# The order of seven Strassen products and their additions, with a PSUM bank as one resource in the plan

## The chip, the cores and the metric

The kernel runs on one core of a Trainium2 chip. The metric is the device time of one execution in microseconds (us). TensorE does the matrix products into PSUM (eight banks of 512 fp32 values in each of 128 partitions), VectorE and ScalarE read and write PSUM and SBUF, GpSimd works on SBUF alone here, and SyncE issues the DMAs.

## What is computed

Linear attention with random features, and then two two-layer perceptrons on its 2304 x 512 result:

```python
k_p, q_p = phi(k * scale), phi(q * scale)          # exp features, 128 of them
kv, z = einsum('bhsm,bhsd->bhmd', k_p, v), k_p.sum(axis=2)
x = (q_p @ kv) / (q_p @ z + 1e-6)                  # 4 x 8 heads, 576 tokens
h = x @ w_in;  x = (h * tanh(softplus(h))) @ w_out     # first perceptron, d_ff 2048
h = x @ w_in2; x = (h * sigmoid(h)) @ w_out2           # second perceptron
```

All inputs and outputs are fp32. Each product runs as three fp32r matmuls on a high and a low part (`mm3`, lines 202 to 205).

## The kernel before

Every instruction is a task of a plan (class `Plan`, lines 69 to 190). A task has an engine, a cost, a due key, names that it reads and writes, and rings of buffers from which it opens new tiles. `order` is a greedy list scheduler: it follows the modelled time, and on the engine that can start first it takes, among the tasks that can start within 0.1 us of that, the one with the lowest key. A reader becomes ready when the last writer's modelled end plus a latency has passed (`LAT`: 0.2 us behind TensorE, 0.15 behind ScalarE and VectorE), a writer behind the last writer and all readers. The list that comes out fixes the order of instructions on every engine. The waits themselves (semaphores) are set afterwards by the tile framework from the tiles' real accesses, not by the plan.

The tokens go in blocks of 256. In the first stretch (attention and phase 0, up to about 395 us) the products `h`, `y`, `kpj`, `qpj` and others run without Strassen. From then on each block of 512 tokens (phases 1 to 4) goes through pairs of 128-wide slices of d_ff. One pair is a step, `step(s, st)` from line 698. Its first layer is a 2 x 2 Strassen-Winograd product: seven products instead of eight, each of six 256-column matmuls (lines 734 to 744), with additions afterwards. A step uses:

- bank A (`ha`) and bank B (`hb`), each 512 columns wide, left half 0 and right half 1; the ring `h4` has four banks, so two steps fit;
- `u`, a tile in SBUF (named `Lfz` in the trace, after the space that it reuses);
- `uz` (ScalarE, line 765): copies B's right half to `u` 0; `ua`, `ub`, `uc`, `ud`, `ue` (VectorE, line 759): u0 += A left; u1 = u0 + B left; B right = u1 + A right; A right = u0 + A right; B left = u0 + B left;
- `act` (lines 705 to 710): the activation `e` (ScalarE, L707), its high part `gh` (ScalarE, L708), its low part `gl` (VectorE, L709), for A and for B; `gh` and `gl` have two buffers each;
- the second layer `Y` (lines 785 to 820): four pieces for a step, two for A's half and two for B's, each of six 512-column matmuls into the `y` banks (a ring of four other banks). Evacuation at a block's end is L841 or L843.

Products are called by their operand number v: in the names of the plan product 4 of step 7 is `Ma7.4`. Before the change the plan's names for what a product writes are `ha:0`, `ha:1`, `hb:0`, `hb:1`, that is, one for each half. Keys: products 0, 4, 5, 3 have the step's key, products 1, 2, 6 with `ud`, `ue` and the activations 0.6 more, `Y` 2.6 more (and an offset of 1.1 for `Y`); the next step's key is 1.9 higher. The last block of 256 tokens has its own branch (`N == 256`, lines 746 to 753) with four products into one bank.

Beside the steps, weights of later pairs are converted and split (`to_f32` and `conv_pair`: ScalarE L612 and L632, VectorE L614 to L618 and L651, GpSimd L633), and the operands of each block are loaded and combined (`load_x`: DMA, VectorE L877).

Of the kernel before, what the change touches and what calls it, by code (L numbers as in the profile page):

```python
# [13 lines left out]
ALU = mybir.AluOpType  # L14
# [179 lines left out]
def performer_two_mlps(ctx: ExitStack, tc: tile.TileContext, qin, kin, omT, w1, w2, out):  # L194
    nc = tc.nc
    PE, ACT, DVE, POOL = nc.tensor, nc.scalar, nc.vector, nc.gpsimd
# [5 lines left out]
    def mm3(o, s_hi, s_lo, m_hi, m_lo, first, last):  # L202
        PE.matmul(o, s_hi, m_hi, start=first, stop=False, skip_group_check=True)  # L203
        PE.matmul(o, s_lo, m_hi, start=False, stop=False, skip_group_check=True)  # L204
        PE.matmul(o, s_hi, m_lo, start=False, stop=last, skip_group_check=True)  # L205
# [61 lines left out]
    T = plan.add  # L267
# [59 lines left out]
    def om_prep():  # L327
# [6 lines left out]
      new=[("cst", "cst")], lat=D)  # L334
# [363 lines left out]
    def step(s, st):  # L698
        ph, N, s_ = st["ph"], st["N"], st["key"]
        pair = "p" in st  # L700
        gh, gl = [f"gh{s}.{x}" for x in range(2)], [f"gl{s}.{x}" for x in range(2)]
        AFN = AF.Mish if ph < 2 else AF.Silu
        tab = "M" if ph < 2 else "S"

        def act(x, h, res, ks):
            e = f"e{s}.{x}"
            T(f"X{s}.{x}", "ACT", 0.6, ks, lambda: ACT.activation(t[e], t[h], AFN), reads=res, writes=[e], new=[(e, "e")], tab=tab)  # L707
            T(f"gh{s}.{x}", "ACT", 0.62, ks, lambda: ACT.copy(t[gh[x]], t[e]), reads=[e], writes=[gh[x]], new=[(gh[x], "ghi")])  # L708
            T(f"gl{s}.{x}", "DVE", 0.69, ks, lambda: DVE.tensor_tensor(t[gl[x]], t[e], t[gh[x]].bitcast(F32), ALU.subtract),  # L709
              reads=[e, gh[x]], writes=[gl[x]], new=[(gl[x], "glo")])  # L710

        if not pair:
            h, X = f"h{s}", f"X{st['bi']}"
            xres = [f"{X}:{x}{g}" for x in "hl" for g in range(2)]

            def H(f, k):
                whi, wlo = [ap() for _, ap in wt_[f, 0]]
                for c in range(NCC):
                    mm3(t[h][:, k * N:(k + 1) * N], whi[:, c * P:(c + 1) * P], wlo[:, c * P:(c + 1) * P], t[X][:, 0, c, :], t[X][:, 1, c, :],
                        c == 0, c == NCC - 1)  # L720

            for k, f in enumerate(st["fs"]):
                T(f"H{s}.{k}", "PE", 1.41, s_, lambda f=f, k=k: H(f, k), reads=xres + [x for x, _ in wt_[f, 0]],
                  writes=[h], new=[(h, "h")] if not k else [])
            act(0, h, [h], s_)
            g_of = [(0, k * N) for k in range(2)]
            wout = [([x for x, _ in wt_[f, 1]], lambda f=f: [ap() for _, ap in wt_[f, 1]]) for f in st["fs"]]
        else:
            p = st["p"]
            V = [f"V{p}.{v}" for v in range(7)]  # L730
            xv = f"x{min(ph, 3) if ph < 4 else 4}.{st['bi']}."
            wout = [([f"O{p}.{x}h", f"O{p}.{x}l"], lambda x=x: [t[f"O{p}.{x}h"], t[f"O{p}.{x}l"]]) for x in range(2)]

            def product(o, v, b, first, last):

                m = [t[xv + b + x].rearrange("p (c t) -> p c t", t=256) for x in "hl"]
                for c in range(2):
                    mm3(o, t[V[v]][:, c * P:(c + 1) * P], t[V[v]][:, 256 + c * P:256 + (c + 1) * P], m[0][:, c, :], m[1][:, c, :],
                        first and c == 0, last and c == 1)

            def M(nm, h, x, v, b, first, last, new, ks, extra=()):
                T(f"M{nm}{s}.{v}", "PE", 0.703, ks, lambda: product(t[h][:, x * 256:(x + 1) * 256], v, b, first, last),
                  reads=[V[v] + ":h", V[v] + ":l", xv + b + "h", xv + b + "l"], writes=[f"{h}:{x}"],
                  new=[(h, "h4")] if new else [], after=extra)

            if N == 256:
                h = f"h{s}"
                M("a", h, 0, 0, "11", True, False, True, s_, ["att"])
                M("a", h, 0, 1, "21", False, True, False, s_)
                M("a", h, 1, 3, "11", False, False, False, s_, [f"Ma{s}.0"])  # L750
                M("a", h, 1, 2, "T", False, True, False, s_)
                act(0, h, [h + ":0", h + ":1"], s_)
                g_of = [(0, k * N) for k in range(2)]
            else:
                A, B, u = f"ha{s}", f"hb{s}", f"u{s}"
                q = lambda r, x: t[r][:, x * 256:(x + 1) * 256]

                def add(nm, o, ox, a, ax, b, bx, ks, new=()):
                    T(f"{nm}{s}", "DVE", 0.42, ks, lambda: DVE.tensor_tensor(q(o, ox), q(a, ax), q(b, bx), ALU.add),  # L759
                      reads=[r for r in (f"{a}:{ax}", f"{b}:{bx}") if r != f"{o}:{ox}"], writes=[f"{o}:{ox}"], new=list(new))  # L760


                M("a", A, 0, 0, "11", True, False, True, s_, ["att"])
                M("a", B, 1, 4, "T2", True, True, True, s_)
                T(f"uz{s}", "ACT", 0.37, s_, lambda: ACT.copy(q(u, 0), q(B, 1)), reads=[B + ":1"], writes=[u + ":0"], new=[(u, "u")])
                add("ua", u, 0, u, 0, A, 0, s_)
                M("a", B, 0, 5, "T3", False, False, False, s_, [f"Ma{s}.4"])
                add("ub", u, 1, u, 0, B, 0, s_)
                M("a", A, 1, 3, "T1", False, False, False, s_, [f"Ma{s}.0"])
                add("uc", B, 1, u, 1, A, 1, s_)  # L770
                M("b", A, 0, 1, "21", False, True, False, s_ + 0.6)
                M("b", B, 0, 2, "T4", False, True, False, s_ + 0.6)
                M("b", A, 1, 6, "22", False, True, False, s_ + 0.6)
                add("ud", A, 1, u, 0, A, 1, s_ + 0.6)
                act(0, A, [A + ":0", A + ":1"], s_ + 0.6)
                add("ue", B, 0, u, 0, B, 0, s_ + 0.6)
                act(1, B, [B + ":0", B + ":1"], s_ + 0.6)
                g_of = [(0, 0), (1, 0)]

        tail = s == len(steps) - 1  # L780
        nb = NCC if tail or (ph == 4 and N == 256) else NCC * N // DM
        Y_ = [f"y{ph}.{st['bi']}.{i}" for i in range(nb)]
        epb = NCC // nb

        def Y(k, cs):
            whi, wlo = wout[k][1]()
            x, off = g_of[k]
            for c in cs:
                y = t[Y_[c // epb]][:, (c % epb) * N:(c % epb + 1) * N]
                mm3(y, whi[:, c * P:(c + 1) * P], wlo[:, c * P:(c + 1) * P], t[gh[x]][:, off:off + N], t[gl[x]][:, off:off + N],  # L790
                    st["first"] and k == 0 and c % epb == 0, st["last"] and k == 1)

        gres = [[gh[g_of[k][0]], gl[g_of[k][0]]] for k in range(2)]
        ky = s_ + (1.6 if N == 256 else 2.6)
        yring = "y0" if ph == 0 else "y"
        att = ["att"] if st["first"] and ph else []

        def YT(nm, ks, cs, new, after=()):
            ys = sorted({Y_[c // epb] for c in cs})
            cost = len(ks) * len(cs) * 3 * (0.117 if N == 256 else 0.2315)  # L800
            T(nm, "PE", cost, ky, lambda: [Y(k, cs) for k in ks], reads=[r for k in ks for r in gres[k] + wout[k][0]],
              writes=ys, new=[(y, yring) for y in ys] if new else [], after=list(after) + att)

        if st["last"]:
            for half in range(2):
                cs = (2 * half, 2 * half + 1)
                if N == 512 or tail:
                    for c in cs:
                        YT(f"Y{s}.{c}", (0, 1), (c,), st["first"])
                else:  # L810
                    YT(f"Y{s}.{half}", (0, 1), cs, st["first"])
                for y in sorted({Y_[c // epb] for c in cs}):
                    evac(s, st, y, Y_.index(y), epb)
        elif N == 256:
            for half in range(2):
                YT(f"Y{s}.{half}", (0, 1), (2 * half, 2 * half + 1), st["first"])
        else:
            for k in range(2):
                for half in range(2):
                    YT(f"Y{s}.{k}{half}", (k,), (2 * half, 2 * half + 1), st["first"] and not k)  # L820
# [180 lines left out]
```

## Time and profile before

| | us |
|---|---|
| median of three runs | 1016.17 (1013.45 to 1018.31) |
| the profiled execution, its own time | 1016.34 |
| its span, first to last instruction | 1014.5 |
| busy: TensorE / VectorE / ScalarE / GpSimd | 965.7 / 614.1 / 527.4 / 398.6 |
| mean granted TensorE clock | 0.979 of full speed |

The span is what the page divides into; the execution's own time is 1.8 us longer. A line of the page or of a view gives the engine, the line of the kernel, the operation, the tiles (written <- read) and times. "Idle before" is the time in which the engine did nothing ahead of an instruction, with what released it. Matmuls overlap: the bar of a 256-column matmul is 0.28 us long while the next one starts 0.12 us later, so distances between starts tell more than bars. PEld is TensorE's weight load.

### The profile page before, as it was taken

What the parts mean: (1) busy time and instruction counts of PE and PEld (TensorE: products, weight loads), DVE (VectorE), ACT (ScalarE), POOL (GpSimd) and SP (SyncE); (2) the same over time, 40 slices, a digit from 0 to 9 for tenths busy, and PEclk for the clock granted to TensorE, in tenths of its full rate; (3) what the DMA queues carried; (4) which work ended last, traced back from release to release, by engine and by line L of the source; (5) the groups of instructions that cost most, each with busy time, mean ns of one, the idle gap of its engine ahead of it and who ended that gap; (6) DMA issues with size and microseconds to landing.
All of it is one profiled execution on the core that took longest, in us unless ns stands there. A gap on an engine that the chain in (4) does not pass through costs nothing.

```text
span 1014.5 us, 18027 instructions
## 1 busy us (share of the span) xinstructions
PE 965.7 (95%) x6628; PEld 889.6 (88%) x6628; DVE 614.1 (61%) x1395; ACT 527.4 (52%) x1139; POOL 398.6 (39%) x526
## 2 busy tenths in 40 slices
PE   8788999999999999999999998999999999999998
PEld 6677899999999999898998887788988988888888
DVE  5799786657877468743653859744438754353422
ACT  4696777678786545532334455534336435333221
POOL 5788564335453355330413365503125323112100
PEclk7799899999999999999999999999999999999999
DMA  7667434323313333513320344332113301230202
GB/s 264 196 186 225 123 93 135 120 62 126 105 53 105 94 104 105 159 70 126 105 73 32 109 142 146 104 104 65 51 32 104 94 2 67 72 112 11 83 1 83
DMA packets 50360, 102.56 MB, mean 101 GB/s; under 512 B 4960, under 2 KB 17504, under 8 KB 50272
## 3 DMA queue, kind: packets, MB, share of 16 engines
q1 hardware_dynamic: 50272, 101.41, 31.6%
q8 instruction: 52, 0.85, 0.4%
q14 instruction: 36, 0.29, 0.1%
HBM read 78.85 MB, written 22.54 MB: 100 GB/s over the span
## 4 chain that ended last, share of the span: by engine, by line
PE 86%; DVE 7%; issue 2%; DMA 1%; ACT 1%; POOL 1%; SPq 0%; DVEq 0%; ACTq 0%; POOLq 0%
PE y L205 12%; PE y L204 12%; PE y L203 12%; PE ha L203 5%; PE h L203 4%; PE h L204 4%; PE h L205 4%; PE ha L204 4%; PE ha L205 4%; PE hb L203 3%; PE acc L422 3%; PE hb L205 3%; PE hb L204 3%; PE kpj L411 3%; DMA kin<-in_kin_dram 1%
## 5 line engine op out<-in xcount | busy, mean ns | idle before, releaser
L709 DVE TENSOR_TENSOR gl<-e,gh 128x512 fp32r<-128x512 f32 x144 | 107.7, 754 | 163.8 <-ACT gh L708 153.3
L203 PE MATMUL y<-gh,W 128*128 128x256 f32 (+1 forms) x528 | 172.1, 326 | 0.2 <-DVE stg L841 0.2
L204 PE MATMUL y<-gh,W 128*128 128x256 f32 (+1 forms) x528 | 171.0, 324 | 0.0
L205 PE MATMUL y<-gl,W 128*128 128x256 f32 (+1 forms) x528 | 170.9, 324 | 0.0
L708 ACT CAST gh<-e 128x512 fp32r<-128x512 f32 x144 | 88.7, 622 | 106.8 <-PE y L204 105.2
L205 PEld LDWEIGHTS y<-gl,W 128*128 128x128 f32 x528 | 99.7, 189 | 8.8
L203 PEld LDWEIGHTS y<-gh,W 128*128 128x128 f32 x528 | 99.7, 189 | 7.2 <-DVE stg L841 0.4
L204 PEld LDWEIGHTS y<-gh,W 128*128 128x128 f32 x528 | 99.7, 189 | 6.7
L203 PE MATMUL h<-X,W 128*128 128x256 f32 x288 | 83.7, 291 | 0.4 <-ACT e L707 0.4
L707 ACT ACTIVATE e<-hb 128x512 f32<-128x512 f32 x48 | 28.7, 598 | 106.2 <-DVE hb L759 106.1
L205 PE MATMUL h<-X,W 128*128 128x256 f32 x288 | 81.5, 283 | 0.0
L204 PE MATMUL h<-X,W 128*128 128x256 f32 x288 | 81.5, 283 | 0.0
L633 POOL TENSOR_TENSOR LX<-Lqf,LX 128x512 fp32r<-128x512 f32 x19 | 26.2, 1383 | 109.0 <-ACT LX L632 79.2
L612 ACT ACTIVATE wa<-wr 128x512 f32<-128x512 f32 x64 | 43.2, 678 | 49.5 <-DVE wt L618 36.8
L616 DVE SCALAR_TENSOR_TENSOR wt<-wr,wt 128x512 int32<-128x512 int32 x64 | 55.8, 872 | 0.5
L203 PEld LDWEIGHTS h<-X,W 128*128 128x128 f32 x288 | 55.0, 191 | 0.8 <-ACT e L707 0.6
L411 PE MATMUL kpj<-cst,kin 128*128 128x256 f32 x144 | 45.0, 448 | 10.7 <-DMA kin<-in_kin_dram 8.2
L204 PEld LDWEIGHTS h<-X,W 128*128 128x128 f32 x288 | 55.0, 191 | 0.2
L205 PEld LDWEIGHTS h<-X,W 128*128 128x128 f32 x288 | 54.9, 191 | 0.2 <-DVE X L595 0.2
L618 DVE SCALAR_TENSOR_TENSOR wt<-wa,wt 128x512 int32<-128x512 int32 x64 | 52.0, 815 | 0.4
L633 POOL TENSOR_TENSOR W<-wt,W 128x256 fp32r<-128x256 f32 (+1 forms) x31 | 33.8, 1100 | 44.4 <-ACT W L632 41.3
L422 PEld LDWEIGHTS acc<-kin,kf 128*128 128x128 f32 (+1 forms) x320 | 44.7, 219 | 5.0 <-ACT kf L384 2.9
(637 smaller groups left out, 3079.7 us busy)
## 6 DMA issues: line engine op xcount, KB each, us to landing
wr<-in_w_dram SPq DMA_DIRECT2D x64, 512.0 KB, 4.0
kin<-in_kin_dram SPq DMA_DIRECT2D x35, 386.0 KB, 3.6
qin<-in_qin_dram SPq DMA_DIRECT2D x36, 256.0 KB, 2.8
xf<-sx SPq DMA_DIRECT2D x18, 256.0 KB, 2.3
yp<-stg SPq DMA_DIRECT2D x18, 256.0 KB, 2.3
stg<-yp SPq DMA_DIRECT2D x18, 256.0 KB, 5.0
y<-stg SPq DMA_DIRECT2D x18, 256.0 KB, 2.7
Lqin<-y SPq DMA_DIRECT2D x18, 256.0 KB, 4.5
```

Of the source, the lines that this page charges most:

```text
L203: PE.matmul(o, s_hi, m_hi, start=first, stop=False, skip_group_check=True)
L204: PE.matmul(o, s_lo, m_hi, start=False, stop=False, skip_group_check=True)
L205: PE.matmul(o, s_hi, m_lo, start=False, stop=last, skip_group_check=True)
L411: PE.matmul(t[pj][:, jj * 256:(jj + 1) * 256], t[res][:, jj * P:(jj + 1) * P], t["cst"][:, P:P + 256], start=True, stop=True, skip_group_c ...
L422: PE.matmul(a[:, h, :], t[f][r0:r1, h * NF:(h + 1) * NF], v[r0:r1, h, :], start=first and h == 0, stop=last, skip_group_check=True)
L612: T("wm" + c, "ACT", 0.62, key, lambda: ACT.activation(t[wa], t[raw][:, :, 1].bitcast(F32), AF.Copy, scale=2.0 ** -112), reads=[raw], writ ...
L616: T("wo" + c, "DVE", 0.95, key, lambda: DVE.scalar_tensor_tensor(t[wt], t[raw][:, :, 0], 29, t[wt], ALU.logical_shift_right, ALU.bitwise_o ...
L618: T("ws" + c, "DVE", 0.8, key, lambda: DVE.scalar_tensor_tensor(t[wt], t[wa].bitcast(I32), 3, t[wt], ALU.logical_shift_left, ALU.bitwise_o ...
L633: T(f"sl{nm}", "Pool", 0.1 + 1.3 * n / DM, key, lambda: POOL.tensor_tensor(lo(), src(), hi().bitcast(F32), ALU.subtract), reads=res + [rh] ...
L707: T(f"X{s}.{x}", "ACT", 0.6, ks, lambda: ACT.activation(t[e], t[h], AFN), reads=res, writes=[e], new=[(e, "e")], tab=tab)
L708: T(f"gh{s}.{x}", "ACT", 0.62, ks, lambda: ACT.copy(t[gh[x]], t[e]), reads=[e], writes=[gh[x]], new=[(gh[x], "ghi")])
L709: T(f"gl{s}.{x}", "DVE", 0.69, ks, lambda: DVE.tensor_tensor(t[gl[x]], t[e], t[gh[x]].bitcast(F32), ALU.subtract), reads=[e, gh[x]], write ...
```

## The change

The plan's name for what a product writes becomes the bank as a whole (`ha` or `hb`), in the additions as well (only `u` keeps its halves). The products are inserted in another order: 4 and 5 into B, 0 and 3 into A, then `uz`, `ua`, `ub`, `uc`, then 6 and 1 into A, `ud` and A's activation, then 2 into B, `ue` and B's activation. The first product to clear bank B is still 4, and the first to clear bank A is still 0. The cost of an addition in the plan goes from 0.42 to 0.43. The branch for 256 tokens keeps its order and takes the whole bank as its name.

```diff
-                  ..., writes=[f"{h}:{x}"],
+                  ..., writes=[h],
...
-                act(0, h, [h + ":0", h + ":1"], s_)
+                act(0, h, [h], s_)
...
+                res = lambda r, x: f"{u}:{x}" if r == u else r
...
-                    T(f"{nm}{s}", "DVE", 0.42, ks, ...
-                      reads=[r for r in (f"{a}:{ax}", f"{b}:{bx}") if r != f"{o}:{ox}"], writes=[f"{o}:{ox}"], new=list(new))
+                    T(f"{nm}{s}", "DVE", 0.43, ks, ...
+                      reads=[r for r in (res(a, ax), res(b, bx)) if r != res(o, ox)], writes=[res(o, ox)], new=list(new))
+                M("a", B, 1, 4, "T2", True, True, True, s_, ["att"])
+                M("a", B, 0, 5, "T3", False, False, False, s_)
                 M("a", A, 0, 0, "11", True, False, True, s_, ["att"])
-                M("a", B, 1, 4, "T2", True, True, True, s_)
-                T(f"uz{s}", "ACT", 0.37, s_, ..., reads=[B + ":1"], writes=[u + ":0"], new=[(u, "u")])
+                M("a", A, 1, 3, "T1", False, False, False, s_)
+                T(f"uz{s}", "ACT", 0.37, s_, ..., reads=[B], writes=[u + ":0"], new=[(u, "u")])
                 add("ua", u, 0, u, 0, A, 0, s_)
-                M("a", B, 0, 5, "T3", False, False, False, s_, [f"Ma{s}.4"])
                 add("ub", u, 1, u, 0, B, 0, s_)
-                M("a", A, 1, 3, "T1", False, False, False, s_, [f"Ma{s}.0"])
                 add("uc", B, 1, u, 1, A, 1, s_)
+                M("b", A, 1, 6, "22", False, True, False, s_ + 0.6)
                 M("b", A, 0, 1, "21", False, True, False, s_ + 0.6)
+                add("ud", A, 1, u, 0, A, 1, s_ + 0.6)
+                act(0, A, [A], s_ + 0.6)
                 M("b", B, 0, 2, "T4", False, True, False, s_ + 0.6)
-                M("b", A, 1, 6, "22", False, True, False, s_ + 0.6)
-                add("ud", A, 1, u, 0, A, 1, s_ + 0.6)
-                act(0, A, [A + ":0", A + ":1"], s_ + 0.6)
                 add("ue", B, 0, u, 0, B, 0, s_ + 0.6)
-                act(1, B, [B + ":0", B + ":1"], s_ + 0.6)
+                act(1, B, [B], s_ + 0.6)
```

## Rows read from the trace of the kernel before

**Rows 1.** The page: its span, and busy time by engine.

```profile
span 1014.5 us, 18027 instructions
PE 965.7 (95%) x6628; PEld 889.6 (88%) x6628; DVE 614.1 (61%) x1395; ACT 527.4 (52%) x1139; POOL 398.6 (39%) x526
```

**Rows 2.** Busy time by stretch; the first line names the columns.

```profile
core 0: us, PE busy (x) PEld busy (x) DVE busy (x) ACT busy (x) POOL busy (x), PEclk, DMA share, GB/s
...
395.00:600.00 205.00, 198.37 (x1293) 179.36 (x1292) 119.08 (x202) 84.99 (x163) 71.56 (x62) 1.00 0.31 97
600.00:655.00 55.00, 48.68 (x286) 42.26 (x285) 47.66 (x74) 30.29 (x60) 34.97 (x29) 0.97 0.40 129
655.00:980.00 325.00, 315.75 (x1981) 280.93 (x1981) 155.35 (x272) 128.91 (x239) 81.00 (x67) 1.00 0.20 64
```

**Rows 3.** Waits of TensorE's matmuls, 395 to 1015: us, times, longest.

```profile
PE ha L203 <- DVE hb L759: 10.3, 20, 0.5
PE ha L203 <- DVE Lfz L759: 5.9, 4, 2.2
PE hb L203 <- DVE hb L759: 4.1, 8, 0.5
PE hb L203 <- ACT e L707: 1.1, 1, 1.1
```

**Rows 4.** Waits of TensorE's weight loads, 395 to 1015.

```profile
PEld ha L203 <- DVE hb L759: 16.0, 21, 1.0
...
PEld hb L203 <- DVE hb L759: 6.9, 10, 0.9
```

**Rows 5.** Line 759, addition ua: count, duration ns minimum/median/maximum, first and last start.

```profile
L759 DVE TENSOR_TENSOR Lfz<-Lfz,ha x48: 402/421/423, 398.9 to 973.8; 128x256 f32<-128x256 f32 x48
```

**Rows 6.** TensorE in order of time, 742.2 to 743.4: start, duration, instruction, idle before.

```profile
742.24 0.28 PE L204 MATMUL hb<-LHL,Lom 128*128 128x256 f32 x1
742.36 0.28 PE L205 MATMUL hb<-LHL,Lom 128*128 128x256 f32 x1
743.16 0.39 PE L203 MATMUL ha<-LX,LFT 128*128 128x256 f32 x1 [0.52 <-DVE hb L759]
743.38 0.28 PE L204 MATMUL ha<-LX,LFT 128*128 128x256 f32 x1
```

**Rows 7.** VectorE in the same stretch: ub, uc.

```profile
741.14 0.42 DVE L759 TENSOR_TENSOR Lfz<-Lfz,hb 128x256 f32<-128x256 f32 x1 [0.25 <-PE hb L205]
742.67 0.43 DVE L759 TENSOR_TENSOR hb<-Lfz,ha 128x256 f32<-128x256 f32 x1 [1.11 <-PE hb L205]
```

**Rows 8.** TensorE at the start of product 1, same step.

```profile
740.94 0.39 PE L203 MATMUL ha<-Lz,Lkv 128*128 128x256 f32 x1
741.16 0.28 PE L204 MATMUL ha<-Lz,Lkv 128*128 128x256 f32 x1
```

**Rows 9.** TensorE, a second-layer piece and product 6 of another step.

```profile
885.00 0.40 PE L203 MATMUL y<-gh,Lz 128*128 128x512 f32 x1
...
886.17 0.40 PE L205 MATMUL y<-gl,Lz 128*128 128x512 f32 x1
887.07 0.38 PE L203 MATMUL ha<-LX,Lkv 128*128 128x256 f32 x1 [0.50 <-DVE hb L759]
```

**Rows 10.** VectorE around it: a gl of the step before, uc.

```profile
882.75 0.69 DVE L709 TENSOR_TENSOR gl<-e,gh 128x512 fp32r<-128x512 f32 x1 [2.05 <-ACT gh L708]
...
886.59 0.43 DVE L759 TENSOR_TENSOR hb<-Lfz,ha 128x256 f32<-128x256 f32 x1
```

**Rows 11.** ScalarE around it: uz.

```profile
885.20 0.37 ACT L765 COPY Lfz<-hb 128x256 f32<-128x256 f32 x1 [0.88 <-PE hb L205]
```

**Rows 12.** TensorE behind the longest wait of the Strassen steps.

```profile
650.47 0.39 PE L203 MATMUL ha<-LX,W 128*128 128x256 f32 x1 [2.16 <-DVE Lfz L759]
...
651.60 0.63 PE L204 MATMUL y<-gh,W 128*128 128x512 f32 x1
652.02 0.63 PE L205 MATMUL y<-gl,W 128*128 128x512 f32 x1
```

More of the change, by code (lines that the diff above doesn't have):

```diff
@@ L742, in M @@
                 T(f"M{nm}{s}.{v}", "PE", 0.703, ks, lambda: product(t[h][:, x * 256:(x + 1) * 256], v, b, first, last),
-                  reads=[V[v] + ":h", V[v] + ":l", xv + b + "h", xv + b + "l"], writes=[f"{h}:{x}"],
+                  reads=[V[v] + ":h", V[v] + ":l", xv + b + "h", xv + b + "l"], writes=[h],
                   new=[(h, "h4")] if new else [], after=extra)
@@ L756, in step @@
                 q = lambda r, x: t[r][:, x * 256:(x + 1) * 256]
+                res = lambda r, x: f"{u}:{x}" if r == u else r
                 def add(nm, o, ox, a, ax, b, bx, ks, new=()):
-                    T(f"{nm}{s}", "DVE", 0.42, ks, lambda: DVE.tensor_tensor(q(o, ox), q(a, ax), q(b, bx), ALU.add),
-                      reads=[r for r in (f"{a}:{ax}", f"{b}:{bx}") if r != f"{o}:{ox}"], writes=[f"{o}:{ox}"], new=list(new))
+                    T(f"{nm}{s}", "DVE", 0.43, ks, lambda: DVE.tensor_tensor(q(o, ox), q(a, ax), q(b, bx), ALU.add),
+                      reads=[r for r in (res(a, ax), res(b, bx)) if r != res(o, ox)], writes=[res(o, ox)], new=list(new))
+                M("a", B, 1, 4, "T2", True, True, True, s_, ["att"])
+                M("a", B, 0, 5, "T3", False, False, False, s_)
                 M("a", A, 0, 0, "11", True, False, True, s_, ["att"])
-                M("a", B, 1, 4, "T2", True, True, True, s_)
-                T(f"uz{s}", "ACT", 0.37, s_, lambda: ACT.copy(q(u, 0), q(B, 1)), reads=[B + ":1"], writes=[u + ":0"], new=[(u, "u")])
+                M("a", A, 1, 3, "T1", False, False, False, s_)
+                T(f"uz{s}", "ACT", 0.37, s_, lambda: ACT.copy(q(u, 0), q(B, 1)), reads=[B], writes=[u + ":0"], new=[(u, "u")])
                 add("ua", u, 0, u, 0, A, 0, s_)
-                M("a", B, 0, 5, "T3", False, False, False, s_, [f"Ma{s}.4"])
                 add("ub", u, 1, u, 0, B, 0, s_)
-                M("a", A, 1, 3, "T1", False, False, False, s_, [f"Ma{s}.0"])
                 add("uc", B, 1, u, 1, A, 1, s_)
+                M("b", A, 1, 6, "22", False, True, False, s_ + 0.6)
                 M("b", A, 0, 1, "21", False, True, False, s_ + 0.6)
+                add("ud", A, 1, u, 0, A, 1, s_ + 0.6)
+                act(0, A, [A], s_ + 0.6)
                 M("b", B, 0, 2, "T4", False, True, False, s_ + 0.6)
-                M("b", A, 1, 6, "22", False, True, False, s_ + 0.6)
-                add("ud", A, 1, u, 0, A, 1, s_ + 0.6)
-                act(0, A, [A + ":0", A + ":1"], s_ + 0.6)
                 add("ue", B, 0, u, 0, B, 0, s_ + 0.6)
-                act(1, B, [B + ":0", B + ":1"], s_ + 0.6)
+                act(1, B, [B], s_ + 0.6)
                 g_of = [(0, 0), (1, 0)]
```

## The prediction, made blind

> **What bounds the kernel now.** I read the page's busy line first: TensorE is busy 965.7 of 1014.5 us, and no other engine is above 614 [rows 1]. A kernel like this gets shorter only where TensorE waits. The table of stretches then says where it waits near the change: the Strassen steps start at about 395 us and the last ends near 980 (their first addition ua starts at 398.9, the last at 973.8 [rows 5]); ahead of 395 there is nothing that the diff touches. In 395 to 600 TensorE is idle 6.6 us, in 655 to 980 9.3 us, at full clock and with VectorE busy 58% and 48% of the time; in 600 to 655, where VectorE is busy 47.7 of 55 us, it is idle 6.3 us [rows 2]. The waits by releaser name two causes [rows 3]. The first is regular: 28 waits (20 + 8), none above 0.5 us, all ended by an addition that writes bank B. That is uc, which reads `u` and A's right half and writes B's right half. The second is irregular: four waits for `ua` or `ub` (5.9 us) and one for an activation (1.1 us).
>
> One instance shows the mechanism. The last matmul of product 2 starts at 742.36, the next product (number 6, into A's right half) only at 743.16 [rows 6]. It needs uc, and uc started at 742.67, after VectorE had sat idle 1.11 us until TensorE's product in bank B had ended; ub, the last thing that uc needs by data, began at 741.14 and took 0.42 [rows 7]. So uc was ready about 1.1 us earlier and was held back by product 2, which writes the *other half of the same bank*. The plan counts halves as separate, so it put product 2 ahead of uc and thought it free; the semaphores go by the bank. A second form: at 887.07 product 6 waits again 0.50 us [rows 9], and here it is the start of the chain that was late: `uz` reads B's right half but began only at 885.20 [rows 11], right after product 5 had ended in B's left half.
>
> **The price of one wait.** The idle column understates it, because a matmul's bar is longer than the distance to the next one. By starts: 743.16 − 742.36 = 0.80 us where neighbours are 0.12 apart, so 0.68 lost; and the first matmul behind a wait takes 0.22 to the next start instead of 0.12, 0.10 to 0.11 more [rows 6]. Together 0.79 us, times 28 = **22.1 us**. The idle column alone gives 10.3 + 4.1 = 14.4 us [rows 3], which would make the result about 1002 us; the weight loads, which have no such overhang, stand idle 16.0 + 6.9 = 22.9 us for the same releaser [rows 4], and I go with them and with the starts.
>
> The Trainium skill ("Perfetto Trace Analysis", section "Identifying the Most-Contended Engine") says that matmul busy time is a poor measure, because matmuls are pipelined, and points to the weight loads instead. The trace agrees: 14.4 us by the one row, 22.9 us by the other.
>
> **The change, part by part.** No arithmetic is added or removed: the same 48 steps [rows 5], each with seven products, one `uz`, five additions, the same DMAs. What moves is order.
>
> (1) *Whole-bank resources.* The plan can no longer put product 2 between ub and uc, nor product 1 ahead of uc. The held-back uc disappears. Takes away: the 28 waits, −22.1 us. Also 20 short ones that show no idle time, where product 1 starts just as ua has ended (740.94: 0.22 us to the next start, 0.10 too long [rows 8]): product 1 now stands behind product 6 and is released long before; −2.1 us.
>
> (2) *Four products first.* uz now stands behind product 5 (both write B), ua behind product 3. What does the chain cost? The step at 882 already runs in this form (products, all four, then uz): from the fourth product's end, 885.00, to product 6 at 887.07 are 2.07 us, with uz at 885.20 and uc from 886.59 [rows 9 to 11]. One second-layer piece of six 512-column matmuls (885.00 to about 886.4 [rows 9]) lay in it and left 0.50 idle. Two such pieces, about 2.8 us, cover it with 0.7 to spare. The plan's own costs (0.43 + 0.15 for each addition, 0.2 behind a product) put product 6 about 1.9 us behind the fourth product, and a piece at 1.39, so it sees that one piece isn't enough and takes a second. Cost: nothing, while two pieces of the step before are ready; 2.1 us where there is none.
>
> (3) *Are they ready?* They need gl of the step before. In that step the second gl began at 882.75 and took 0.69, so it landed at 883.44, 1.5 us ahead of 885.00 [rows 10]. The ring for gh has two buffers, so that gl follows the piece two steps back; its place does not change. Only the order inside the last three is new: 1 comes last, so ud and A's activation come one product (0.71 us) behind B's. If B's pieces then go first, those for A have two pieces, 2.8 us, more until they are used. I cost it at nothing.
>
> (4) *Queues.* On VectorE ua, ub and uc now stand close together, behind whatever conversion came before; ScalarE's uz likewise. Who waits: product 6, with 0.7 us and more of cover where before it had none. SP's DMAs keep their operations and depend on no bank; GpSimd reads no bank.
>
> (5) *Unknown: the plan is a greedy list, so every later choice may shift.* The trace of before can't show that. From below: the irregular waits. The longest is 2.16 us, and some 3.5 us of lower clock (1.2 GHz) behind it cost more (the 512-column starts are 0.42 apart at 651.60, where six of them took 1.4 us at 885.00, 0.23 each [rows 9, 12]). If all of the irregular ones and this drop went, I would get 5.9 + 1.1 + 0.6 idle, some 3 for the overhang and the clock: about −10. From above: one wait of about 1.2 us (1.05 idle as the smallest of that kind) at each of the 12 block borders, where product 6's operand, which is made last, is now wanted ahead of products 1 and 2: +14. The nearest rows are the five late waits, all in stretches with much conversion work [rows 2, 3], which the change does not touch; I take them as unchanged, and +2 for the borders.
>
> Sum against the profiled execution (1016.3 us, span 1014.5 and 1.8 around it; the median of the runs is 1016.2, so no shift): 1016.3 − 22.1 − 2.1 + 2 = **994 us**. With the ends of (5): 982 to 1006.
>
> **The rivals.**
> *A: half the waits stay or move.* For: the waits in 600 to 655 are VectorE's work, and a wait gone ahead of them only makes TensorE arrive earlier; a plan that finds only one piece ready leaves the 0.5 us of 887.07 [rows 9]. Against: 1.5 us between gl and its use. 14 × 0.79 = 11 stay: 1005 us, between 1001 and 1011.
> *B: no change.* The 28 gaps could be a shortage of banks, with uc only the last to be seen; then order would not help. The place would be a wait for an activation, the last reader of a bank; there is one, of 1.1 us [rows 3]. 1016 us.
> The Trainium skill ("Perfetto Trace Analysis", section "Optimization Strategy") says that the same gap repeating on the engine that should be full can mean too little PSUM for the next tile. Here 28 gaps repeat and one of the waits is for an activation, so the trace speaks for another cause.
> *C: slower.* Both banks are shut from the fourth product to uc. If the step before has no finished piece at that moment, TensorE stands for the whole 2.07 us and 0.11 behind it. The point: gl landing 1.5 us later than at 883.44. Against an average loss before of 24.2 / 48 = 0.5 us, an affected step costs 1.7 us more and an unaffected one gains 0.5; from 11 steps of 48 the kernel is slower than before. With half of the steps: 1016.3 + 24 × 1.7 − 24 × 0.5 = 1045 us. What speaks for it is 600 to 655, where VectorE, which makes gl, is busy 47.7 of 55 us [rows 2]; that is 5 steps, not 11.
> The Trainium skill ("Perfetto Trace Analysis", section "Matmuls") wants independent groups to rotate through the banks, so that one bank is read out under the next group's products; two banks filled together and then read together is the opposite. Whether it matters hangs on the pieces into the four other banks.
>
> **How the numbers follow.** Forecast 0.71, its own range 985 to 1002; A 0.12; B 0.08; C 0.09. Range for 8 in 10: 985 to 1007 (the forecast and most of A). A measurement of this kernel tells 0.5% (5 us) from no change: faster (under 1011) 0.82, same 0.09, slower 0.09.
>
> **What would show it.** Right: the waits of products for additions into bank B fall from 28 to a few; between product 3 and product 6 stand two second-layer pieces in nearly every step; uc follows ub at once; TensorE's idle time in 395 to 980 falls from 22 to about 8 us, most of it around 600 to 655. The price of 0.79 is right if time gained is about 1.6 times the idle time gone. Wrong: waits of a product for uc or uz after one piece (A); a wait of product 4 or 0 for an activation (B); second-layer pieces waiting for gl (C). Wrong altogether if 600 to 655 grows by over 10 us, by conversions placed differently.

## The result: 990.7 us, 2.5% faster

The changed kernel takes 990.7 us (median of four runs, 989.8 to 990.8); the kernel before 1016.8 in the same comparison. The ratio is 0.9746, 95% interval 0.9721 to 0.9771. The profiled execution took 990.8 us, of which the span is 989.0; before 1016.3 and 1014.5 [rows 1].

The waits of TensorE's matmuls from 395 us on, changed kernel (us in total, times, longest; the additions are now on line 760):

```profile
PE hb L203 <- ACT e L707: 3.1, 1, 3.1
PE y L205 <- DVE gl L709: 1.9, 1, 1.9
PE ha L203 <- DVE hb L760: 1.5, 3, 0.6
PE ha L203 <- ACT e L707: 1.1, 2, 0.8
```

Against [rows 3], the 28 waits for an addition into bank B (14.4 us idle) are three (1.5 us), and no product waits for `ua` or `ub`. Busy time by stretch (the columns are those of [rows 2]; the Strassen steps now end near 955):

```profile
395.00:600.00 205.00, 203.21 (x1350) 185.80 (x1349) 129.18 (x212) 90.10 (x177) 79.00 (x68) 1.00 0.33 106
600.00:655.00 55.00, 49.18 (x302) 43.08 (x301) 48.22 (x77) 30.11 (x60) 29.70 (x25) 1.00 0.38 125
655.00:955.00 300.00, 300.00 (x1928) 271.92 (x1927) 150.88 (x261) 122.44 (x231) 81.35 (x67) 1.00 0.20 66
```

From 655 to 955 TensorE has no idle time at all, where before it lost 9.3 us between 655 and 980. Most of what is left sits in the stretch in which VectorE is busy 48.2 of 55 us. TensorE was idle 22.2 us in the three stretches before and is 7.6 us now.

One step of the changed kernel, TensorE (start, duration, instruction, idle before):

```profile
854.64 0.28 PE L205 MATMUL ha<-Lkv,Lkf 128*128 128x256 f32 x1
854.76 0.39 PE L203 MATMUL y<-gh,W 128*128 128x512 f32 x1
...
856.15 0.40 PE L203 MATMUL y<-gh,W 128*128 128x512 f32 x1
...
857.32 0.39 PE L205 MATMUL y<-gl,W 128*128 128x512 f32 x1
857.55 0.28 PE L203 MATMUL ha<-LHL,Lkf 128*128 128x256 f32 x1
```

and VectorE beside it, `ua`, `ub`, `uc`:

```profile
855.03 0.42 DVE L760 TENSOR_TENSOR Lfz<-Lfz,ha 128x256 f32<-128x256 f32 x1 [1.74 <-PE ha L205]
855.48 0.42 DVE L760 TENSOR_TENSOR Lfz<-Lfz,hb 128x256 f32<-128x256 f32 x1
855.94 0.43 DVE L760 TENSOR_TENSOR hb<-Lfz,ha 128x256 f32<-128x256 f32 x1
```

Behind the last matmul of the fourth product two second-layer pieces follow (854.76 and 856.15). uc follows ub at once and ends at 856.37; product 6 starts at 857.55, 1.18 us after uc, and waits for nothing. Counted over TensorE's instructions, two pieces or more stand between the fourth and the fifth product in all 48 steps; before there was none in 24 steps and one in 19.

**The measure used below.** Idle time is too short a measure, so I add up, over TensorE's records from 395 us to the end, the distance between neighbouring starts less what it is in an undisturbed row (0.117 us for 256 columns, 0.232 for 512). Before this loss is 41.1 us, after it 13.3: 27.8 less, in 395 to 600 from 12.1 to 3.8, in 600 to 655 from 10.4 to 7.1, behind 655 from 18.5 to 2.4. Up to 393.9 us TensorE's matmuls stand in the same order in both kernels. In the changed one they start 2.4 us later from 112 us on, and this distance is still 2.4 at 395; over the other kernels below it is 0.8 to 3.1 us at 125 (the largest group of waits there, 8.2 us before and 9.7 in the changed kernel, is for the DMAs of `kin`). Together −27.8 + 2.4 = −25.4, and the spans differ by 25.5. Nothing is left to explain elsewhere.

| kernel | median, us | profiled, us | loss from 395 on, us | profiled − loss |
|---|---|---|---|---|
| before | 1016.8 | 1016.3 | 41.1 | 975 |
| changed | 990.7 | 990.8 | 13.3 | 978 |
| names_only | 999.0 | 999.0 | 22.2 | 977 |
| order_only | 1028.8 | 1028.6 | 52.0 | 977 |
| cost_only | 1017.6 | 1016.9 | 40.9 | 976 |
| edges | 995.5 | 996.1 | 19.2 | 977 |
| no_piece | 999.9 | 1000.6 | 24.0 | 977 |
| cheap_chain | 1008.5 | 1010.9 | 32.6 | 978 |
| uncovered | 1112.6 | 1114.5 | 136.3 | 978 |
| sa_pool | 1010.3 | 1010.3 | 17.2 | 993 |
| xt_pool | 1002.3 | 1002.4 | 25.2 | 977 |
| sa_late | 995.6 | 996.2 | 18.2 | 978 |
| real_costs | 997.6 | 999.7 | 23.8 | 976 |

All but one stand on the same sum, 975 to 978 plus the loss. The exception, sa_pool, falls 16 us behind between 125 and 395.

### The profile page after: what moved, and what is told of

It is laid out like the page before. It is cut to its first block, busy times and chain, and to the rows that moved or that the text cites. A ratio compares the mean times of both kernels' runs of the same rounds, so it can differ in the third digit from the quotient of the medians.

```text
span 989.0 us, 17895 instructions
## 1 busy us (share of the span) xinstructions
PE 953.7 (96%) x6628; PEld 886.6 (90%) x6628; DVE 616.9 (62%) x1395; ACT 523.1 (53%) x1139; POOL 398.7 (40%) x526
## 4 chain that ended last, share of the span: by engine, by line
PE 86%; DVE 6%; issue 2%; DMA 2%; POOL 2%; ACT 2%; SPq 0%; DVEq 0%; POOLq 0%; ACTq 0%
PE y L203 12%; PE y L204 12%; PE y L205 12%; PE h L203 5%; PE h L205 5%; PE h L204 5%; PE ha L203 4%; PE ha L204 4%; PE ha L205 4%; PE acc L422 4%; PE hb L203 3%; PE hb L204 3%; PE hb L205 3%; PE kpj L411 3%; DMA kin<-in_kin_dram 2%
## 5 line engine op out<-in xcount | busy, mean ns | idle before, releaser
L205 PEld LDWEIGHTS y<-gl,W 128*128 128x128 f32 x528 | 99.3, 188 | 11.2 <-DVE gl L709 2.5
L633 POOL TENSOR_TENSOR LX<-Lqin,LX 128x512 fp32r<-128x512 f32 x23 | 31.7, 1380 | 137.1 <-ACT LX L632 107.0
L760 DVE TENSOR_TENSOR hb<-Lfz,hb 128x256 f32<-128x256 f32 x48 | 20.5, 426 | 77.7 <-PE hb L205 77.5
L633 POOL TENSOR_TENSOR LX<-Lqf,LX 128x512 fp32r<-128x512 f32 x15 | 20.7, 1385 | 101.2 <-PE ha L204 52.1
L616 DVE SCALAR_TENSOR_TENSOR wt<-wr,wt 128x512 int32<-128x512 int32 x64 | 58.3, 911 | 0.6
L707 ACT ACTIVATE e<-h 128x512 f32<-128x512 f32 x48 | 28.1, 598 | 47.2 <-PE h L205 47.0
```

The costliest lines, as they stand in the source:

```text
L616: T("wo" + c, "DVE", 0.95, key, lambda: DVE.scalar_tensor_tensor(t[wt], t[raw][:, :, 0], 29, t[wt], ALU.logical_shift_right, ALU.bitwise_o ...
L633: T(f"sl{nm}", "Pool", 0.1 + 1.3 * n / DM, key, lambda: POOL.tensor_tensor(lo(), src(), hi().bitcast(F32), ALU.subtract), reads=res + [rh] ...
L760: T(f"{nm}{s}", "DVE", 0.43, ks, lambda: DVE.tensor_tensor(q(o, ox), q(a, ax), q(b, bx), ALU.add), reads=[r for r in (res(a, ax), res(b, b ...
```

## The experiments

### Is it the names, the order, or a lucky plan?

**names_only**: the names of the change, the order of insertion of before.

```diff
-  # 4, 5, 0, 3, uz, ua, ub, uc, 6, 1, ud, act A, 2, ue, act B   (writes=[h])
+  # 0, 4, uz, ua, 5, ub, 3, uc, 1, 2, 6, ud, act A, ue, act B   (writes=[h])
```

> The changed kernel with the products and additions inserted in the order of the kernel before (0, 4, uz, ua, 5, ub, 3, uc, 1, 2, 6), so that only the whole-bank names are left of the change. Theory (the plan was wrong about what waits for what, and the names put that right): the 28 waits for uc of the kernel before are gone here too, at most 8 waits of a product for an addition; since the chain now alternates between products and additions (3 only behind ua), a few waits more than in the changed kernel; 994 us (989 to 1003). Rival (it is the order, four products first, that gains): no gain or a loss, 1010 to 1030. Rival (any other plan would have been as good: luck of a greedy list): anything from 1005 to 1020.

Measured: 999.0 us, ratio to before 0.9833 (0.9815 to 0.9852), twelve waits, two of them for uc. The names alone give 18 of the 26 us. The chain with products between the additions opens two gaps in a step instead of one, and of the 8.9 us that it loses more than the changed kernel 5.3 fall between 590 and 655, where VectorE is behind: its waits between 590 and 625 (us, times, longest) begin with

```profile
PE ha L203 <- DVE Lfz L760: 2.9, 2, 2.2
PE hb L203 <- ACT e L707: 2.0, 1, 2.0
```

**order_only**: the order of the change, a name for each half.

```diff
-                  ..., writes=[h],
+                  ..., writes=[f"{h}:{x}"],
...
-                T(f"uz{s}", "ACT", 0.37, s_, ..., reads=[B], ...)
+                T(f"uz{s}", "ACT", 0.37, s_, ..., reads=[B + ":1"], ...)
```

> The changed kernel with a name for each half, as before; the order of insertion (4, 5, 0, 3, uz, ua, ub, uc, 6, 1, ud, 2, ue) is that of the change. Theory: without the names the plan still believes that product 2 may go ahead of uc and that uz may start behind product 4, the order in the program text only breaks ties; 20 to 35 waits of a product for uc come back, 1014 us (1006 to 1020). Rival (order): 991 us (988 to 997), few waits.

Measured: 1028.8 us, ratio 1.0125 (1.0108 to 1.0142): 12 us slower than before, and outside what I had expected.

```profile
PE hb L203 <- DVE hb L759: 11.7, 22, 0.7
PE ha L203 <- DVE Lfz L759: 11.1, 12, 1.3
PE ha L203 <- DVE hb L759: 3.9, 7, 0.8
```

The 29 waits for uc are back as expected. The twelve for ua I had not foreseen. One of them:

```profile
892.54 0.42 DVE L759 TENSOR_TENSOR Lfz<-Lfz,ha 128x256 f32<-128x256 f32 x1 [1.38 <-ACT Lfz L767]
...
893.02 0.39 PE L203 MATMUL ha<-LFT,Lom 128*128 128x256 f32 x1 [0.92 <-DVE Lfz L759]
```

ua waited for uz, since product 5 had been put between product 4 and uz, into the same bank; a product into bank A waits for ua. It is the same error of the plan in another place. So this order in the program text, with the false names, is no gain by itself.

**cost_only**: the kernel before with 0.43 for an addition.

```diff
-                    T(f"{nm}{s}", "DVE", 0.42, ks, ...
+                    T(f"{nm}{s}", "DVE", 0.43, ks, ...
```

> The kernel before with the plan's cost of an addition at 0.43 in place of 0.42, nothing else. It shows what a reshuffled plan without a reason gives. Theory: waits for uc stay at 22 to 34, 1016 us (1011 to 1021). Rival (luck): 5 us or more away from 1016.

Measured: 1017.6 us, ratio 1.0011 (0.9992 to 1.003), 28 waits for uc. The cost in the plan is not the cause. As a test of luck it says little, since the list hardly moved: of TensorE's 6628 matmuls 30 stand at another place than before. The other runs say more. In order_only 2130 matmuls stand at another place than before and in edges (below) 2118, two reshuffles of one size; the one that keeps the false names loses 12 us, the other gains 21. Nor did the scheduler find a better list by its own account: the time that the plan models for itself (`self.span` in `order`) is 978.1 us before, 978.1 for names_only, 976.2 for order_only, 975.0 for edges and 975.3 for the changed kernel.

**edges**: the kernel before with two edges more.

```diff
-                M("b", A, 0, 1, "21", False, True, False, s_ + 0.6)
-                M("b", B, 0, 2, "T4", False, True, False, s_ + 0.6)
+                M("b", A, 0, 1, "21", False, True, False, s_ + 0.6, [f"uc{s}"])
+                M("b", B, 0, 2, "T4", False, True, False, s_ + 0.6, [f"uc{s}"])
```

> The kernel before, with half names and its order, and two edges in the plan more: products 1 and 2 come behind uc. Theory: of the 28 waits 18 follow directly on a product (uc held back by product 1 or 2 in its bank) and 10 follow on a second-layer piece (uz held back by product 5); the edges take away the first kind alone: some 10 waits left, 18 x 0.79 = 14 us and some 2 of the short ones less, 1001 us (995 to 1008). Rival (luck or order): 1010 to 1020, with the number of waits not going with the kind.

Measured: 995.5 us, ratio 0.9783 (0.9747 to 0.982), four waits for uc. The first kind went as the theory says; the second kind went too, against what I wrote. A plan that knows that nothing of products 1, 2 and 6 may run before uc has to put pieces there, and they cover a late uz as well: between the fourth and fifth product at least one piece stands in 47 of 48 steps, where before 24 steps had none. So 21 of the 26 us hang on what the two edges tell the plan: products 1 and 2 shut the banks that uc needs. The two were not tried one at a time. In the kernel before 14 of the 18 waits of the first kind stand behind product 2, in the bank that uc writes [rows 6, 7], and four directly behind product 1, in bank A, whose other half uc reads; uc in one of these four:

```profile
465.70 0.43 DVE L759 TENSOR_TENSOR hb<-Lfz,ha 128x256 f32<-128x256 f32 x1 [1.06 <-PE ha L205]
```

Edges and names_only, two ways of telling the plan, differ by 3.5 us.

### What does the chain cost where it is not covered?

**no_piece**: the pieces of the step before come behind products 1 and 2.

```diff
         step(s, st)
+        if f"Mb{s}.1" in plan.index:
+            for nm, i in list(plan.index.items()):
+                if nm.startswith(f"Y{s - 1}."):
+                    plan.tasks[i]["deps"] |= {plan.index[f"Mb{s}.1"], plan.index[f"Mb{s}.2"]}
```

> The changed kernel with one dependency more in the plan: the second-layer pieces of the step before come only behind products 1 and 2, so that nothing stands between the four products and product 6. It measures what the chain costs uncovered, the price of rival C. In the changed kernel the fourth product of a step ends at 854.76 and uc at 856.37: product 6 could start at about 856.42, 1.66 us behind, and its first matmul takes 0.11 more. Theory (two pieces in the gap are what makes the four-products-first order cost nothing): 48 steps x 1.77 = 85 us more, 1075 us (1055 to 1090), 45 or more waits of a product for uc of 1.4 to 1.7 us each. Rival (the order is good by itself and the pieces are not needed, since the chain overlaps the products): under 1010 us.

Measured: 999.9 us (ratio 0.9822, 0.978 to 0.9864). My number was far off, and neither reading was tested: with four banks the plan found other cover. In 41 of the 48 steps no piece but three to five products of a neighbouring step stand in the gap, so that two steps run interleaved. Nine waits for uc remain (11.7 us).

**uncovered**: the same with two banks instead of four, so that this cover is gone.

```diff
-    ring("h4", ["P0", "P1", "P2", "P3"], BANK, F32, ps)
+    ring("h4", ["P0", "P1"], BANK, F32, ps)
```

> The kernel no_piece (pieces of the step before only behind products 1 and 2) with two banks in place of four for the first layer, so that the plan can't put the next step's four products into the gap either, as it did in no_piece. Now nothing is left to stand between the fourth product and product 6. Theory (price of the chain, from the changed kernel: 1.66 us to product 6 and 0.11 behind it): 48 steps x 1.77 = 85 us more than the changed kernel, 1076 us (1060 to 1085), 45 or more waits for uc of 1.4 to 1.7 us idle. Rival (the chain costs less since the additions overlap the products): under 1040 us.

Measured: 1112.6 us, ratio 1.093 (1.0876 to 1.0984), 122 us above the changed kernel. All 48 steps wait for uc, 27 of them with 1.5 us idle, as worked out:

```profile
1009.79 0.28 PE L205 MATMUL ha<-LHL,Lkf 128*128 128x256 f32 x1
1011.57 0.39 PE L203 MATMUL ha<-LX,Lkv 128*128 128x256 f32 x1 [1.50 <-DVE hb L760]
1011.79 0.28 PE L204 MATMUL ha<-LX,Lkv 128*128 128x256 f32 x1
1011.91 0.28 PE L205 MATMUL ha<-LX,Lkv 128*128 128x256 f32 x1
```

1.78 us between starts instead of 0.12, and 0.22 to the next: 1.66 + 0.11 = 1.77 us lost. The other 21 are longer: in most of them other VectorE work stands between the additions, in a few uz on ScalarE comes late, and nothing hides it any more. By starts all 48 lose 110 us. And behind some of the longer waits the clock falls, which my 85 us had left out:

```profile
579.84 0.58 PE L203 MATMUL ha<-LHL,Lzb 128*128 128x256 f32 x1 [2.45 <-DVE hb L760]
580.22 0.42 PE L204 MATMUL ha<-LHL,Lzb 128*128 128x256 f32 x1
580.44 0.41 PE L205 MATMUL ha<-LHL,Lzb 128*128 128x256 f32 x1
580.65 0.41 PE L203 MATMUL ha<-LHL,Lzb 128*128 128x256 f32 x1
```

Behind this wait of 2.45 us the 256-column starts are 0.21 apart instead of 0.12, the lower of the two clock levels (1.2 GHz); over 395 to 1090 the granted clock is 0.96 instead of 1.00.

**cheap_chain**: the plan takes ua, ub and uc for 0.1 us.

```diff
-                    T(f"{nm}{s}", "DVE", 0.43, ks, ...
+                    T(f"{nm}{s}", "DVE", 0.1 if nm in ("ua", "ub", "uc") else 0.43, ks, ...
```

> The changed kernel in which the plan takes ua, ub and uc for 0.1 us each in place of 0.43, so that it believes that one second-layer piece (1.39) covers the chain. The chip needs 1.66 us behind the fourth product. Theory (the gain hangs on the plan's costs being near the chip's): one piece in most gaps, 30 to 48 waits for uc of 0.1 to 0.3 us idle, each 0.27 + 0.11 lost, 1005 us (998 to 1012). Rival (the costs do not matter once the banks are right): 991 us (988 to 996).

Measured: 1008.5 us, ratio 0.9925 (0.989 to 0.9959); about as expected. In 30 steps the plan put one piece into the gap, and 29 waits for uc are of the size that the price says (0.10 to 0.22 us idle, most of them too short to be listed as waits); the clearest:

```profile
871.89 0.40 PE L205 MATMUL y<-gl,W 128*128 128x512 f32 x1
872.39 0.39 PE L203 MATMUL ha<-Lkv,Lkf 128*128 128x256 f32 x1
872.62 0.28 PE L204 MATMUL ha<-Lkv,Lkf 128*128 128x256 f32 x1
```

0.50 us between starts instead of 0.23 and 0.23 instead of 0.12: 0.38 lost, with an idle time of 0.1. By starts the 29 waits lose some 12 of the 19 us that this kernel loses more than the changed one. The time also holds nine longer waits for uc, up to 3.1 us, of which my price knew nothing. So the second piece is what makes the changed order free, and the plan takes it because its 0.43 is near the chip's 0.42.

### What is left: VectorE between 600 and 645

**sa_pool**: the additions of the weight pairs on GpSimd.

```diff
-            T(f"sa{p}.{x}", "DVE", 0.42, ks, lambda: DVE.tensor_tensor(...
+            T(f"sa{p}.{x}", "Pool", 0.75, ks, lambda: POOL.tensor_tensor(...
```

> The changed kernel with the four additions of a weight pair (L651, VectorE, 0.41 us each) on GpSimd. What is left of TensorE's loss in the changed kernel lies around 600 to 645, where VectorE is busy 43.6 of 45 us. Theory (VectorE is the bound there): three pairs fall into it, 12 additions, 5 us of VectorE less, 2 to 4 us of TensorE's waits less, 988 us (985 to 991). Rival (GpSimd work beside VectorE's stretches VectorE's own instructions, as L614 with a mean of 0.90 us in this stretch against 0.41 elsewhere shows, so that it gives nothing): 991 us or more, to 995.

Measured: 1010.3 us (ratio 0.9938, 0.9906 to 0.997). Most of the loss is not in the stretch in question: between 125 and 395 TensorE is busy 257.8 us against 267.8 in the changed kernel, while the first pairs are converted beside the attention. (The 0.41 of L614 in what I expected is its time with no GpSimd work beside it; outside 600 to 655 its mean is 0.57.) **sa_late** moves the pairs 5 to 11 alone.

```diff
+            T(f"sa{p}.{x}", *(("Pool", 0.75) if p > 4 else ("DVE", 0.42)), ks, lambda: (POOL if p > 4 else DVE).tensor_tensor(...
```

> The changed kernel with the additions of the weight pairs 5 to 11 alone (L651) on GpSimd; the plan up to 560 us stays as in the changed kernel, which sa_pool did not leave alone (it lost 16 us of TensorE time between 125 and 395). Theory (VectorE is the bound in 600 to 645): 988 us (985 to 991). Rival (GpSimd's work stretches VectorE's, nothing gained): 990 to 995 us.

Measured: 995.6 us (989.4 to 996.2; ratio 0.9777, 0.9735 to 0.9818), loss 18.2 us. No gain. **xt_pool** moves the subtractions of the block operands.

```diff
-            T("xt" + x, "DVE", 0.68, ks, lambda: DVE.tensor_tensor(...
+            T("xt" + x, "Pool", 1.42, ks, lambda: POOL.tensor_tensor(...
```

> The changed kernel with the subtractions that combine the operands of a block (L877 before, four in a block of 512 tokens, VectorE 0.68 to 1.79 us) on GpSimd. Theory (VectorE is the bound in 600 to 645): one or two blocks load there, 3 to 8 us of VectorE less, 988 us (984 to 991). Rival (stretching, or the longer chain on GpSimd, whose split of the operands comes behind it): 991 to 1000 us, waits of the first products of a block for operands.

Measured: 1002.3 us (ratio 0.9861, 0.9829 to 0.9892), loss 25.2. No gain either. **real_costs** tells the plan the durations that the trace shows in that stretch.

```diff
-        T("wb" + c, "DVE", 0.7, ...
+        T("wb" + c, "DVE", 0.9 if l == 1 and f < 8 else 0.7, ...
...
-            T(f"gl{s}.{x}", "DVE", 0.69, ...
+            T(f"gl{s}.{x}", "DVE", 0.98 if pair and 69 < st["key"] < 79 else 0.69, ...
```

(and in the same way L616 with 1.05 and the block subtractions with 1.2)

> The changed kernel with the plan's costs nearer to what the trace shows in its busiest VectorE stretch (600 to 645): L614 0.90 in place of 0.70 and L616 1.05 in place of 0.95 for the pairs 4 to 7, gl 0.98 in place of 0.69 and the operand subtractions 1.2 in place of 0.68 for the steps and blocks there. Theory (the waits that are left come from the plan's too low costs there): 3 to 6 of the 9 us lost in 600 to 645 go, 986 us (984 to 989). Rival (VectorE's work itself is the bound there, so another order gains nothing): 990 to 996 us.

Measured: 997.6 us (ratio 0.9813, 0.9763 to 0.9863). A single wait is larger than all that it might have saved:

```profile
617.79 0.41 DVE L760 TENSOR_TENSOR Lfz<-Lfz,ha 128x256 f32<-128x256 f32 x1
...
620.59 0.42 DVE L760 TENSOR_TENSOR hb<-Lfz,ha 128x256 f32<-128x256 f32 x1
...
621.06 0.58 PE L203 MATMUL ha<-LFT,W 128*128 128x256 f32 x1 [7.95 <-DVE hb L760]
```

ua stood behind more than five microseconds of conversions and subtractions in VectorE's queue, two more conversions stood between the additions, and no piece lay in the gap.

Four attempts, none better than the changed kernel. That VectorE is busy there is seen; that TensorE's loss goes with how busy it is, is not: in sa_late VectorE's busy time between 600 and 645 fell from 43.6 to 39.0 us, and TensorE's loss between 600 and 655 rose from 7.1 to 11.2. The traces do show that GpSimd's work stretches VectorE's. In the changed kernel the 101 gl with no GpSimd instruction beside them take 0.68 to 0.70 us, and the 12 that have one beside them almost throughout take 1.26 on average, up to 1.79; the additions of a step, which read PSUM, take 0.42 either way. TensorE's wait for gl in the changed kernel comes behind such a one (GpSimd, VectorE, TensorE):

```profile
639.99 1.71 POOL L633 TENSOR_TENSOR LHL<-Lqin,LHL 128x512 fp32r<-128x512 f32 x1
640.50 1.75 DVE L709 TENSOR_TENSOR gl<-e,gh 128x512 fp32r<-128x512 f32 x1
642.30 0.50 PE L205 MATMUL y<-gl,W 128*128 128x512 f32 x1 [1.89 <-DVE gl L709]
```

So work moved to GpSimd comes back in part on VectorE. How much of each attempt's loss is that, and how much the plan's choices, none of these runs separates. This stays open, and 7 us at most hang on it.

## Why the prediction was right, point by point

*What bounds the kernel, and the mechanism.* Right. A plan with half names puts products 1 and 2 into the banks that uc needs; edges takes away that alone and gets 21 us, order_only keeps the false names and gets none. The Trainium skill ("PSUM — Partial Sum Buffer", section "PSUM bank collisions raise a hardware error") says that accesses have to be guarded by bank (and quadrant) and not by address. The trace agrees for what the framework's waits do: VectorE stood idle 1.11 us ahead of uc until a product in the other half had ended [rows 7].

*The price of a wait, 0.79 us.* Right: by starts the 28 waits lost 21.9 us. In form too: uncovered shows 1.50 us idle for 1.77 lost, cheap_chain 0.1 idle for 0.38 lost. Idle time is short by 0.27 for every wait, however long the wait is. Time gained over idle time gone came to 27.8 / 14.6 = 1.9, not 1.6, since the 20 short waits and the stretch at the lower clock had little or no idle time to begin with. Two readings on the way were wrong without harm to the sum. The wait at 887.07 [rows 9] is ahead of product 1 and not 6 (the order in that step is 1, 2, 6), but it too is for uc. And the weight loads do overhang: their bars are 0.19 us long with starts 0.12 apart (742.12 and 742.24), so that their 22.9 us, of 31 waits, is near the 21.9 partly by chance.

*Terms of the sum.* The 28 waits, −22.1: three are left, which cost 2.0 us and 0.3 behind them, so some −20 with them. The 20 short ones, −2.1: gone. The borders, +2: the size came, by luck, since it is these same 2.3 us, at 404, 555 and 645, where a block's first step stands. The reason that I gave, product 6 waiting for its operand, did not come; product 6 waits for uc, and uc for other VectorE work around the additions (at 404 conversions of weights, at 555 subtractions of operands, at 645 the late gl above, a subtraction and a conversion). The first:

```profile
404.19 0.39 PE L203 MATMUL ha<-Lkv,Lzb 128*128 128x256 f32 x1 [0.64 <-DVE hb L760]
```

*The mis-sized term* is the irregular waits, which I took as unchanged. They and the small rest fell by about 6 us (41.1 − 21.9 − 2.1 = 17.1 before, 13.3 − 2.3 = 11.0 now). The waits of 1.05 and 0.92 us for `ua` at 399 and 475 are gone, and so is the one of 2.16 us at 650 with the lower clock behind it [rows 12]; at 615 there is one of 3.1 us, now for an activation. Cover that is there for the regular chain seems to catch VectorE also when it is late; no run shows that by itself. My lower end of part (5), −10, was nearer than the 0 that I chose. The first 125 us, with the same matmuls, took 2.4 us more in this execution, which offset part of it. The rest is within 0.5 us of the sum, and so 994 became 990.8.

*Cover and readiness.* Two pieces or more in every gap: right, and by uncovered and cheap_chain it is what counts. gl came in time but once, the 1.9 us at 642, which I had at nothing. *Rival A* is what cheap_chain brings about: 1008.5, near my 1005. *Rival B* fell with edges, which leaves banks and buffers as they were; of its sign there is something, since the waits of products 0 and 4 for an activation rose from one (1.1 us) to three (4.2 us in all). *Rival C* had the price nearly right for one step (2.07 + 0.11 against 1.77, since the fourth product is now in bank A and uz runs beside it), but its point was wrong: with no piece ready the plan doesn't stand still, it takes another step's products, in the two other banks (no_piece, 999.9). It needs two things to fail at once; with 48 steps uncovered the kernel takes 122 us more, not the 85 us of the price, because other VectorE work and the clock come on top.

## What to carry to other kernels

If a scheduler's resources are finer than what the program's waits go by, it takes for free what then waits on the chip: look for one wait of the same length at the same place in many steps, and ask what its releaser itself was waiting for. Tell the plan the coarse truth first (two edges gave 21 of 26 us); the order inside the step is worth less, and without the truth it can lose. Price a wait on TensorE by starts of matmuls, not by idle time, and count in a plan what covers each chain: one piece too few cost less than half a microsecond here, no cover at all 1.8 or more.

## What the runs showed of the hardware that I had not expected

A matmul that had to wait costs 0.16 us ahead of it (the overlap that it no longer has) and 0.11 us behind it, even where the profile shows next to no idle time: 0.38 us lost at 872.39 for a wait that is idle 0.1.

Idle times of 2.16 us before [rows 12] and of 2.45 us in uncovered (579.84) were followed by the lower clock level; the waits of 1.50 us at the end of uncovered were not (granted clock 1.00 from 1000 to 1090). The length of the idle time alone does not decide it: in uncovered 2.46 us at 416.85 was not followed by it (granted clock 1.00 from 410 to 429), and in the changed kernel 3.13 us at 615 was not either, the starts are 0.12 apart at once and the granted clock is 1.00 over the whole stretch:

```profile
615.25 0.39 PE L203 MATMUL hb<-LX,W 128*128 128x256 f32 x1 [3.13 <-ACT e L707]
615.47 0.28 PE L204 MATMUL hb<-LX,W 128*128 128x256 f32 x1
615.59 0.28 PE L205 MATMUL hb<-LX,W 128*128 128x256 f32 x1
```

No run was made to find out what does. Nor had I expected that GpSimd's work lengthens VectorE's instructions on SBUF (gl from 0.69 us to as much as 1.79) and not the additions that read PSUM (0.42 either way).
